# Moving row loads, combinations and first-stage pieces at the end of a kernel's ramp

## The chip, the cores and the metric

The kernel runs on one core of one Trainium2 chip. The metric is device microseconds of one execution. A core has a matrix engine (TensorE, PE in the profile), a vector engine (VectorE, DVE), a scalar engine (ScalarE, ACT), GpSimd (POOL) and a sync engine (SyncE, SP) that only issues transfers. ScalarE and GpSimd issue transfers too, each through its own queue. Each engine works its instructions off in order and waits for others by semaphores. TensorE writes to PSUM; the others work from PSUM or SBUF, except GpSimd, which in this kernel works from SBUF to SBUF.

## The reference

Two blocks follow each other. The first is a global filter: a real Fourier transform along the sequence of 3008, a product with a complex filter per frequency and channel, and the inverse transform. The second is a gated two-layer network on 24064 tokens.

```python
B, S, C, D_FF = 8, 3008, 256, 2048
X = np.fft.rfft(x, axis=1)                       # x: (8, 3008, 256)
y = np.fft.irfft(X * (filt_r + 1j * filt_i), n=S, axis=1)
t = y.reshape(B * S, C)
h = t @ w_in                                     # (24064, 2048)
out = (h * (1 / (1 + np.exp(-h)))) @ w_out       # (24064, 256)
```

`w_in` and `w_out` arrive as 64-bit floats (each is a float32 array times a numpy float64 scalar), so the kernel has to turn their words into 32-bit floats itself.

## The kernel before

**Transform.** S is split as 47 times 64 and the transform of each of the eight batches runs in stages on TensorE: a first stage over 94 rows (matmuls into tiles named pa, or pf for later batches), a twiddle stage (`forward`, tiles pb), the filter product on VectorE (`products`), an inverse twiddle stage (`inverse`, tiles pc) and a last stage (`stage3`, tiles pd) that leaves y with channels in partitions. Between stages the data is turned round through memory in HBM: the tiles q go out to d2 and come back as the tile t4, which `stage3` reads. For batch 0 that tile is a part of the not yet used weight tile w_t. Its rows come in three pieces, `load_t4_rows(k)` for k = 0, 1, 2, two transfers of 256 KB each; piece k needs the q stores of groups 2k and 2k+1. Group 4 is produced last.

**Network.** Both matrix products use a seven-product scheme on 2 by 2 blocks. A pair is 512 (or 480) tokens; each pair takes eight steps, one for each double block jp of the weights. `hidden(step)` gives seven matmuls (tiles px, pyz), copies of px to abc and the gating to g; `project(step - 1)` gives seven matmuls from g into acc. A loop over steps and eight rounds hands them out alternately, and `put(step, round, ...)` places every other piece of work into that sequence. With matmuls alone a step takes about 6.1 us, 14 matmuls of 0.43 us. The whole order of instructions is thus written out by hand; each engine gets its own in-order stream from it. Transfers by SP and ScalarE take one of eight completion semaphores in turn, and one that takes a semaphore still in use first waits for the earlier transfer on it, whichever queue that was on. GpSimd's transfers have another eight.

**Weights.** For each of the 16 weight blocks j, `weights` loads 512 KB of 64-bit words. `split` takes exponent and mantissa bits apart (two VectorE tensor_scalar instructions) and converts them (two ScalarE activations, four for j = 0, 2, 6), `rounded` rounds and sets the sign (three on VectorE), `placed` multiplies both into w_t. For each pair of blocks, `combine_weights` forms the sums of the seven-product scheme: four instructions of 256 elements per partition, on VectorE.

**The ramp.** Everything before step 0 is the ramp: transform of batch 0 and weight blocks 0 to 8. Its end is the stretch of the script from `inverse(2)` on: groups 3, 5 and 4 of the inverse stage, then the first two of eight first-stage pieces of batch 1 (`second["stage1"](u, False)`, tile pa, two 512-wide matmuls each, evicted by ScalarE and stored by GpSimd in `store_rows`), then 14 filler matmuls (`idle_wide`) whose result nobody reads, then `stage3` for groups 0 to 3. The other six first-stage pieces stand in steps 1 to 6. A one-column copy by GpSimd into the tile `gate` keeps the two row stores behind the placing of block 8.

In the steps, weight block j (9 to 15) has split, rounding and, for some, a combination after round 1 of step j - 9, and placing after round 5. The first-stage piece of batch 1 stands after round 3. Outputs go out through SP.

Of the kernel before, what the change touches and what calls it, by code (L numbers as in the profile page):

```python
# [46 lines left out]
FP32 = mybir.dt.float32  # L47
U32 = mybir.dt.uint32
AFT = mybir.ActivationFunctionType
ALU = mybir.AluOpType  # L50
# [120 lines left out]
def kernel(  # L171
# [59 lines left out]
    gate = cpool.tile([128, 1], FP32)  # L231
    x_all = xpool.tile([128, 2, 2, 2 * C], FP32)
    x_t = [x_all[:, i] for i in range(2)]

# [33 lines left out]
    def spectral(b):  # L268
# [257 lines left out]
        def rows_first(g):  # L526

            if g in (2, 3):
                room = t4pool.tile([128, 4, C], FP32, name=f"q_{b}_{g}", tag="t4")
                tiles = room[:, 0:2], room[:, 2:4]  # L530
            else:
                tiles = [pool.tile([128, 2, C], FP32, name=f"q_{b}_{g}_{i}", tag=tag) for i, (pool, tag) in
                         enumerate(((zpool, "z"),) * 2 if g == NG - 1 else ((qpool, "q"), (opool, "o")))]
            for i, qt in enumerate(tiles):
                copy, queue = (nc.scalar.copy, nc.scalar) if i == 0 or g < 4 else (nc.vector.tensor_copy, nc.sync)
                copy(out=qt, in_=halves[g][i])
                a0 = 8 * g + 4 * i
                queue.dma_start(out=d2[a0:a0 + 4].rearrange("a n h c -> (a n) h c"), in_=qt)
# [19 lines left out]
            for h in range(2):  # L558
                nc.sync.dma_start(out=t4s[g][64 * h:64 * h + 2 * NS], in_=d2[:, 4 * g:4 * g + 4, h, :])

        def load_t4_rows(k):

            first, by = SPREAD[k]
            for h in range(2):
                nc.sync.dma_start(out=us["t4"][64 * h + first:64 * h + first + 15 * by + 1:by],
                                  in_=d2[16 * k:16 * k + 16, 0:16, h, :])

        def stage3(g, home=None):
# [48 lines left out]
    def plan(b, part):  # L617
# [1 line left out]
        at = STEPS * b  # L619

        if b == 1:
            for u in range(2, 8):
                put(at + u - 49, 3, part["stage1"], u)
        else:
            put(at - 72, 0, part["reverse_x"])
            for f, step, load, places in ((0, -56, -66, ((-60, 3), (-60, 5), (-59, 5), (-58, 5))),
# [299 lines left out]
    def split_weights(*js):  # L926

        for j in js:
            words = raws[j].rearrange("p w (n t) -> p (w n) t", t=2)
# [8 lines left out]
            else:  # L938
# [5 lines left out]
            raws[j] = lo, hi, e, m, ef, mf, ends[0].bitcast(FP32), ends[1].bitcast(FP32), ends[1]  # L944
            v.tensor_scalar(out=e, in0=hi, scalar1=20, scalar2=0x7ff,
                            op0=ALU.logical_shift_right, op1=ALU.bitwise_and)
            nc.scalar.activation(out=ef, in_=e, func=AFT.Relu, bias=bias_t[:, 0:1])
            v.tensor_scalar(out=m, in0=hi, scalar1=0xfffff, scalar2=None, op0=ALU.bitwise_and)
# [50 lines left out]
    def weights(*js, queue=None):  # L999
        for j in js:  # L1000
            if wide:
                load_weights(j, queue)

    def split(*js):
        if wide:
            split_weights(*js)
# [75 lines left out]
    for k in range(16):  # L1082
        part["stage1_first"](k, 1)
        if k < 12:
            part["stage1_first"](k + 4, 0)
    second["load_x"](0)
    second["load_x"](1)
    weights(6, 7, 8)
    part["forward"](0, fill=4)
    placed(0, 1)  # L1090
    for g in range(1, 4):
# [18 lines left out]
    inverse(1)  # L1110
    products(3)
    part["forward"](5)
    part["load_t4_rows"](0)
    products(4)
    inverse(2)
    products(5)
    inverse(3)
    split(4, 5)
    combine_weights(0)
    inverse(5)  # L1120
    placed(2, 3)
    inverse(4)
    part["load_t4_rows"](1)
    part["load_t4_rows"](2)
    weights(9)
    split(6, 7)
    rounded(4, 5)
    split(8)
    for u in range(2):
        second["stage1"](u, False)  # L1130
    placed(4, 5)
    rounded(6, 7)
    placed(6, 7)
    rounded(8)
    placed(8)
    gp.tensor_copy(out=gate, in_=w_t[:, 4, A11, 0, 0:1])
    for u in range(2):
        second["store_rows"](u)
    idle_wide(14)
    for g in range(4):  # L1140
        part["stage3"](g)
    nc.sync.dma_start(out=wi_t, in_=wi_dram.ap())
    second["load_x"](2)
    weights(10, 11, 12)
    second["load_x"](3)
    weights(13)
    early[0] = None
    plan_rest(0, part)
    for g in (4, 5):
# [86 lines left out]
```

## Time and profile before

| | |
|---|---|
| runs | 2579.97, 2580.51 and 2583.06 us, median 2580.51 |
| profiled execution | 2580.21 us, span 2578.4 us |
| TensorE | 2554.4 us busy (99%), clock granted 0.995 on average |
| VectorE, ScalarE, GpSimd | 1664.1, 1086.4 and 420.2 us busy |
| TensorE from 55.5 to 70 us | 10.03 of 14.5 us busy |
| TensorE from 100 to 140 us | 39.81 of 40 us busy |

In the profile, "L580" is a line of the kernel, "px<-ty,w_t" names the tile written and the tiles read, and "x64" the number of records; a float32 matmul leaves two records. In a timeline each line is start, duration, engine, line, operation and count, and in brackets the idle time before it and what ended it. The chain is the work that ended last, followed back from the end; in order of time it gives start, duration and what. A line for a stretch of time gives the busy time of PE, weight load (PEld), DVE, ACT and POOL with their counts, then the granted TensorE clock (1.00 is full), the share of time in which the DMA engines were busy, and GB/s.

### The profile page before, as it was taken

How to read it: one execution, taken by the hardware profiler on the slowest of the kernel's cores; microseconds unless marked ns; L12 is line 12 of the kernel's file. 1: busy time of each engine (PE TensorE's matmuls, PEld its weight loads, DVE VectorE, ACT ScalarE, POOL GpSimd, SP SyncE). 2: the span in 40 equal slices, each digit the busy share in tenths (PEclk: the TensorE clock that was granted, in tenths of full speed). 3: DMA queues.
4: the chain of work that ended last, by engine and by line, in shares of the span. 5: the costliest groups of instructions: out<-in, count | busy, mean ns of one | idle time of the engine just before them, and what ended most of it. 6: DMA issues, size and time to landing. Idle time of an engine off the chain costs nothing.

```text
span 2578.4 us, 48112 instructions
## 1 busy us (share of the span) xinstructions
PE 2554.4 (99%) x18852; PEld 2197.4 (85%) x18852; DVE 1664.1 (65%) x3587; ACT 1086.4 (42%) x3011; POOL 420.2 (16%) x668
## 2 busy tenths in 40 slices
PE   9899999999999999999999999999999999999998
PEld 6688888888888888888888888988888888888987
DVE  7766666666666666666666666666666666555554
ACT  3544444444444444434444434444444444444443
POOL 2211111121112111311122111211121112101101
PEclk9899999999999999999999999999999999999999
DMA  9521232222222222222223222331232311210011
GB/s 290 159 60 50 71 79 63 60 64 75 60 63 69 70 62 58 76 73 64 64 60 87 51 66 58 80 80 46 66 80 64 73 41 29 63 19 16 9 17 16
DMA packets 200443, 171.08 MB, mean 66 GB/s; under 512 B 122100, under 2 KB 174180, under 8 KB 199428
## 3 DMA queue, kind: packets, MB, share of 16 engines
q1 hardware_dynamic: 179080, 117.85, 19.8%
q0 software_dynamic: 16768, 44.13, 5.4%
q10 hardware_dynamic: 4368, 6.03, 0.8%
q8 instruction: 148, 2.42, 0.4%
q14 instruction: 79, 0.65, 0.1%
HBM read 96.07 MB, written 81.26 MB: 69 GB/s over the span
## 4 chain that ended last, share of the span: by engine, by line
PE 97%; DMA 2%; DVE 0%; ACT 0%; issue 0%; ACTq 0%; SPq 0%; DVEq 0%
PE acc L813 44%; PE px L750 26%; PE pyz L750 19%; PE pd L580 3%; PE pb L457 2%; PE pc L500 2%; PE pf L424 1%; PE pa L344 0%; DMA w_t<-in_x_dram 0%; PE pc L522 0%; DMA w_t<-d 0%; PE pa L335 0%; DMA d_t<-d_tbl 0%; DMA e_t<-e_tbl 0%; DMA filt<-in_filt_r_dram 0%; DMA d<-q 0%
## 5 line engine op out<-in xcount | busy, mean ns | idle before, releaser
L813 PE MATMUL acc<-g,w_t 128*128 128x256 f32 (+1 forms) x5376 | 1508.8, 375 | 0.4 <-DVE g L721 0.4
L813 PEld LDWEIGHTS acc<-g,w_t 128*128 128x128 f32 x5376 | 1021.5, 190 | 115.8 <-DVE g L721 0.8
L721 DVE TENSOR_TENSOR g<-pyz,abc 128x256 f32<-128x256 f32 (+1 forms) x1152 | 479.3, 416 | 621.0 <-ACT abc L771 356.6
L721 DVE TENSOR_TENSOR g<-g 128x256 f32<-128x256 f32 (+3 forms) x1152 | 598.7, 520 | 196.6 <-ACT g L754 183.4
L750 PE MATMUL px<-ty,w_t 128*128 128x256 f32 (+1 forms) x2304 | 679.3, 377 | 1.1 <-ACT abc L765 0.6
L754 ACT ACTIVATE g<-g 128x256 f32<-128x256 f32 (+1 forms) x1152 | 472.9, 410 | 249.7 <-DVE g L721 249.7
L750 PEld LDWEIGHTS px<-ty,w_t 128*128 128x128 f32 x2304 | 432.7, 190 | 65.0 <-issue 6.2
L721 POOL TENSOR_TENSOR s<-s 128x256 f32<-128x256 f32 (+1 forms) x329 | 254.8, 791 | 1416.4 <-DVE s L833 1393.8
L750 PE MATMUL pyz<-y,w_t 128*128 128x256 f32 (+1 forms) x1536 | 454.0, 377 | 0.0
L750 PEld LDWEIGHTS pyz<-y,w_t 128*128 128x128 f32 x1536 | 284.0, 190 | 47.2 <-DVE g L721 7.1
L765 ACT COPY abc<-px 128x256 f32<-128x256 f32 (+1 forms) x384 | 141.1, 368 | 373.0 <-PE px L750 373.0
L771 ACT COPY abc<-px 128x256 f32<-128x256 f32 (+1 forms) x384 | 141.5, 369 | 338.7 <-PE px L750 337.7
L754 ACT ACTIVATE g<-px 128x256 f32<-128x256 f32 (+1 forms) x384 | 145.8, 380 | 300.7 <-PE px L750 300.7
L750 PE MATMUL px<-y,w_t 128*128 128x256 f32 (+1 forms) x768 | 232.6, 385 | 0.8 <-DVE y L594 0.8
L750 PE MATMUL pyz<-ty,w_t 128*128 128x256 f32 (+1 forms) x768 | 225.7, 376 | 0.2 <-DVE g L721 0.2
L750 PEld LDWEIGHTS px<-y,w_t 128*128 128x128 f32 x768 | 140.4, 190 | 33.9 <-DVE y L600 6.7
L750 PEld LDWEIGHTS pyz<-ty,w_t 128*128 128x128 f32 x768 | 144.6, 190 | 18.7 <-DVE g L721 1.0
L758 ACT COPY abc<-px 128x256 f32<-128x256 f32 (+1 forms) x384 | 135.4, 353 | 54.1 <-PE px L750 54.1
L580 PEld LDWEIGHTS pd<-wi_t,t 48*64 48x64 f32 x3840 | 61.2, 135 | 25.9 <-ACT g L754 16.4
L436 POOL DMA_DIRECT2D d<-tf x144 | 71.4, 502 | 37.0 <-DVE tf L432 29.0
L863 DVE STREAM_TRANSPOSE o<-s 128x256 f32<-128x256 f32 x192 | 73.9, 423 | 1.5 <-issue 1.0
L833 ACT COPY s<-acc 128x512 f32<-128x512 f32 (+1 forms) x94 | 54.2, 577 | 47.6 <-PE acc L813 47.6
(136 smaller groups left out, 1261.6 us busy)
## 6 DMA issues: line engine op xcount, KB each, us to landing
t<-d SPq DMA_DIRECT2D x120, 192.0 KB
t<-d SPq DMA_DIRECT2D x84, 256.0 KB
d<-q POOLq DMA_DIRECT2D x84, 256.0 KB, 2.6
out_dram<-o SPq DMA_DIRECT2D x636, 32.0 KB
d<-tf POOLq DMA_DIRECT2D x144, 96.0 KB, 2.9
xr<-in_x_dram SPq DMA_DIRECT2D x6, 1472.0 KB
x_all<-in_x_dram SPq DMA_DIRECT2D x72, 96.0 KB
x_all<-xr SPq DMA_DIRECT2D x72, 96.0 KB
```

The source lines that it names most:

```text
L436: nc.gpsimd.dma_start(out=d1[k // 2, :, k % 2, n0:n0 + 4], in_=us["tf"][32 * k:32 * k + NS].rearrange("p q n c -> p (q n) c"))
L457: nc.tensor.matmul(out=ps[k][32 * j:32 * j + 32, ri, :], lhsT=d_t[rows, 4 * g + at, ri, :], rhs=rhs, start=True, stop=True)
L580: nc.tensor.matmul(out=ps[h][c0:c0 + 64, cb, i, :], lhsT=t4[rows, i, 128 * cb + c0:128 * cb + c0 + 64], rhs=wi_t[rows, :], start=True, sto ...
L721: eng.tensor_tensor(out=out, in0=in0, in1=in1, op=op)
L750: nc.tensor.matmul(out=out, lhsT=w_t[:, jp, c, 0], rhs=rhs, start=start, stop=True, skip_group_check=True)
L754: nc.scalar.activation(out=g[:, k, 0:n], in_=g[:, k, 0:n] if src is None else src, func=AFT.Silu)
L758: nc.scalar.copy(out=sums[:, 0, 0:n], in_=xo)
L765: nc.scalar.copy(out=sums[:, 1, 0:n], in_=xo)
L771: nc.scalar.copy(out=sums[:, 2, 0:n], in_=xo)
L813: nc.tensor.matmul(out=acc[pair][i][:, h, 0:n], lhsT=w_t[:, jp, c, 1], rhs=g[:, k, 0:n], start=(jp == 0 and h == 0), stop=last, skip_group ...
L833: copy(out=s[:, 2 * i:2 * i + 2, 0:n], in_=acc[pair][i][:, :, 0:n])
L863: v.transpose(out=o[:, :, h, :], in_=results[pair][:, ((2, 6), (4, 1))[chunk][h], :])
```

## The change

At the end of the ramp:

- The loads of the first two x pieces of batch 1 and of weight block 8 leave the place before `forward(0)`. Block 8 is loaded with block 9, after the last rows; the x pieces are loaded after `stage3`, where pieces 2 and 3 were.
- The first two first-stage pieces, with their evictions, their stores and `gate`, leave the ramp. All eight pieces of batch 1 now stand after round 3 of steps 1 to 8.
- Rows k = 0 and 1 are issued by GpSimd in place of SP; k = 2 stays on SP.
- Blocks 2 to 5 are placed by GpSimd, and the combinations of pairs 0 to 3 are made by GpSimd.
- `split` falls into `bits` (VectorE) and `converted` (ScalarE), so that the conversions of blocks 4 and 5 stand behind the q copies.
- The second q copy of group 3 goes to VectorE and its store to SP.
- The filler grows from 14 to 22 matmuls.

In the steps:

- Block 8 is prepared in step 0, and all blocks get new places (`turns`): split at a turn, rounding two rounds later, placing four rounds later. The turns are, as step and round, (0, 1), (1, 0), (1, 7), (2, 6), (3, 5), (4, 4), (5, 1) and (6, 0) for blocks 8 to 15.
- The combinations of pairs 4 to 7 are made by GpSimd, four rounds after the turn of the second block.

```diff
-                copy, queue = (nc.scalar.copy, nc.scalar) if i == 0 or g < 4 else (nc.vector.tensor_copy, nc.sync)
+                copy, queue = (nc.scalar.copy, nc.scalar) if i == 0 or g < 3 else (nc.vector.tensor_copy, nc.sync)
...
-        def load_t4_rows(k):
+        def load_t4_rows(k, queue=None):
...
-                nc.sync.dma_start(out=us["t4"][64 * h + first:64 * h + first + 15 * by + 1:by],
+                (queue or nc.sync).dma_start(out=us["t4"][64 * h + first:64 * h + first + 15 * by + 1:by],
...
-            for u in range(2, 8):
-                put(at + u - 49, 3, part["stage1"], u)
+            for u in range(8):
+                put(at + u - 47, 3, part["stage1"], u)
...
-    second["load_x"](0)
-    second["load_x"](1)
-    weights(6, 7, 8)
+    weights(6, 7)
...
-    part["load_t4_rows"](0)
     products(4)
+    combine_weights(0, eng=gp)
     inverse(2)
+    part["load_t4_rows"](0, nc.gpsimd)
     products(5)
     inverse(3)
-    split(4, 5)
-    combine_weights(0)
+    bits(4, 5)
+    placed(2, 3, eng=gp)
+    part["load_t4_rows"](1, nc.gpsimd)
     inverse(5)
-    placed(2, 3)
+    bits(6, 7)
     inverse(4)
-    part["load_t4_rows"](1)
+    converted(4, 5)
     part["load_t4_rows"](2)
-    weights(9)
-    split(6, 7)
+    weights(8, 9)
+    combine_weights(1, eng=gp)
+    converted(6, 7)
     rounded(4, 5)
-    split(8)
-    for u in range(2):
-        second["stage1"](u, False)
-    placed(4, 5)
+    placed(4, 5, eng=gp)
+    combine_weights(2, eng=gp)
     rounded(6, 7)
     placed(6, 7)
-    rounded(8)
-    placed(8)
-    gp.tensor_copy(out=gate, in_=w_t[:, 4, A11, 0, 0:1])
-    for u in range(2):
-        second["store_rows"](u)
-    idle_wide(14)
+    combine_weights(3, eng=gp)
+    idle_wide(22)
     for g in range(4):
         part["stage3"](g)
     nc.sync.dma_start(out=wi_t, in_=wi_dram.ap())
-    second["load_x"](2)
+    second["load_x"](0)
     weights(10, 11, 12)
-    second["load_x"](3)
-    weights(13)
+    second["load_x"](1)
...
-    for j in range(9, NJ):
-        if j < 12:
-            put(j - 9, 1, lambda j=j: (split(j), combine_weights(j - 8), rounded(j)))
-        else:
-            put(j - 9, 1, lambda j=j: (split(j), rounded(j)))
-        put(j - 9, 5, placed, j)
+    turns = {8: (0, 1), 9: (1, 0), 10: (1, 7), 11: (2, 6), 12: (3, 5), 13: (4, 4), 14: (5, 1), 15: (6, 0)}
+    for j, (step, rnd) in turns.items():
+        turn = step * ROUNDS + rnd
+        put(0, turn, split, j)
+        put(0, turn + 2, rounded, j)
+        put(0, turn + 4, placed, j)
         if j % 2:
-            put(*((j - 8, 5) if j < 15 else (j - 9, 6)), combine_weights, j // 2, 0)
-            put(*{13: (j - 8, 7), 15: (j - 8, 1)}.get(j, (j - 7, 5)), combine_weights, j // 2, 1)
-        if j < 11:
-            put(j - 9, 1, weights, j + 5)
+            put(0, turn + 4, lambda jp=j // 2: combine_weights(jp, eng=gp))
+        if j in (8, 9, 10):
+            put(0, turn + 4, weights, j + 5)
```

More of the change, by code (lines that the diff above doesn't have):

```diff
@@ L230 @@
     bias_t = cpool.tile([128, 5], FP32)
-    gate = cpool.tile([128, 1], FP32)
     x_all = xpool.tile([128, 2, 2, 2 * C], FP32)
@@ L924, in load_weights, with bits_of_weights @@
         raws[j] = raw
-    def split_weights(*js):
+    def bits_of_weights(*js):
         for j in js:
@@ L946, in split_weights, with convert_weights @@
                             op0=ALU.logical_shift_right, op1=ALU.bitwise_and)
+            v.tensor_scalar(out=m, in0=hi, scalar1=0xfffff, scalar2=None, op0=ALU.bitwise_and)
+    def convert_weights(*js):
+        for j in js:
+            _, _, e, m, ef, mf, *_ = raws[j]
             nc.scalar.activation(out=ef, in_=e, func=AFT.Relu, bias=bias_t[:, 0:1])
-            v.tensor_scalar(out=m, in0=hi, scalar1=0xfffff, scalar2=None, op0=ALU.bitwise_and)
             nc.scalar.activation(out=mf, in_=m, func=AFT.Identity, scale=2.0 ** -20, bias=1.0)
@@ L1002, in weights, with bits, converted @@
                 load_weights(j, queue)
+    def bits(*js):
+        if wide:
+            bits_of_weights(*js)
+    def converted(*js):
+        if wide:
+            convert_weights(*js)
     def split(*js):
-        if wide:
-            split_weights(*js)
+        bits(*js)
+        converted(*js)
     def rounded(*js):
```

## The prediction

> **What bounds the kernel now.** I read the page first: one core, TensorE (PE) 99% busy, chain 97% PE. So a change near the start is worth the time by which the first dense TensorE stretch moves, less any TensorE work added later. Its table of slices shows one dent, in slice 2. I then asked for the chain in order of time there, and for TensorE's timeline:
>
> ```profile
> PE 97%; DMA 2%; DVE 0%; ACT 0%; issue 0%; ACTq 0%; SPq 0%; DVEq 0%
> ...
> 55.31 5.42 DMA w_t<-d
> 60.81 5.07 DMA d<-q
> 66.61 4.10 DMA w_t<-d
> 70.85 7.12 PE pd L580 x254
> ...
> 59.13 6.21 PE L1037 MATMUL idle<-d_t,wx_t 96*128 96x256 f32 x28
> 69.81 0.42 PE L580 MATMUL pd<-wi_t,w_t 48*64 48x47 f32 x2 [4.47 <-DMA w_t<-d]
> 70.85 7.07 PE L580 MATMUL pd<-wi_t,w_t 48*64 48x47 f32 x254 [0.62 <-DMA w_t<-d]
> 78.69 1.19 PE L750 MATMUL px<-y,w_t 128*128 128x256 f32 x2 [0.77 <-DVE y L594]
> 87.58 0.60 PE L813 MATMUL acc<-g,w_t 128*128 128x256 f32 x2
> ```
>
> Three transfers stand in a row: rows k=0 into w_t, the last q store, rows k=2. TensorE idles from 65.34 to 69.81. ScalarE's timeline says why the store was late, and the stretch by stretch view what the gap does to the clock (column before the DMA share):
>
> ```profile
> 58.25 0.58 ACT L536 COPY q<-pc 128x512 f32<-128x512 f32 x1 [0.40 <-ACT q L536]
> 60.81 0.33 ACTq L538 DMA_DIRECT2D d<-q  x1
> 61.18 0.72 ACT L947 ACTIVATE w_t<-w_t,bias_t 128x512 f32<-128x512 uint32 x1 [2.35 <-DMA w_t<-d]
> ...
> 66.00:67.00 1.00, 0.00 (x0) 0.00 (x0) 1.00 (x2) 1.00 (x4) 0.00 (x0) 1.00 0.00 0
> 68.00:69.00 1.00, 0.00 (x0) 0.00 (x0) 0.90 (x3) 0.00 (x0) 0.00 (x0) 0.50 1.00 276
> 86.00:87.00 1.00, 1.00 (x4) 0.66 (x3) 0.09 (x2) 0.69 (x2) 0.00 (x0) 0.50 1.16 343
> 88.00:89.00 1.00, 1.00 (x6) 0.88 (x5) 0.86 (x2) 0.21 (x1) 0.00 (x0) 1.00 1.06 228
> ```
>
> The copy was done at 58.83, but its store issued at 60.81, when rows k=0 had landed: in the built program both use the same completion semaphore. Finer stretches put the half clock from 67.1 to 87.5. After that TensorE is full: 39.81 of the 40 us from 100 to 140.
>
> **What the Trainium skill says.** "TensorE: Matmul & The Clock Gate", Part 1: the clock halves after an idle window of about 3.4 us that runs free of the kernel, and returns after a busy one. The trace agrees on the free run (67.1 to 87.5 is six windows), not on a whole idle window: it fell 1.8 us after the last matmul. "SBUF — State Buffer", Who interferes with whom: a VectorE instruction with two SBUF inputs, or a tensor_scalar in its fast mode, and a GpSimd instruction that reads SBUF lock each other out for its whole length. The trace agrees: the tensor_scalar at 49.92 took 1.15 us while GpSimd added until 50.79, its like afterwards 0.41. "GPSIMD Engine Reference", 4.1 Engine selection: two-input elementwise work is about twice slower there; here 0.69 to 0.75 against 0.37 us. "DMA: Bandwidth & Descriptors", SWDGE vs HWDGE vs iDMA: GpSimd's DMAs build descriptors in software in SBUF and can be held by VectorE's fast mode. No run yet shows such a row load; the d<-q stores by POOL land in 2.6 us, the nearest row.
>
> **The change part by part**, against the profiled execution (span 2578.4, its time 2580.2; the median, 2580.51, is 2.1 above the span).
>
> (a) Fewer loads before the rows. x 0 and 1 (768 KB) and weight block 8 (512 KB) leave SP's queue at 39 to 50. ScalarE's store of q_1_0 waited 3.3 us there for an x load (issue at 49.22 after a copy done at 45.92); that goes. TensorE still ends pc at about 55.5: GpSimd's additions end at 50.79 as before.
>
> (b) Store order. q_4_0's store needs no rows load any more: pc ends 55.6, copy 0.6, issue about 56.3 in place of 60.81. But q_4_1, on VectorE and then SP, now follows bits(6,7), four tensor_scalars of 0.41, while GpSimd places blocks 2 and 3. Bounds: VectorE always first, copy done at 57; GpSimd always first, at 59.7. I take 58.4. Landing 2.6 later, 61.0. The second store of q_3 also goes to VectorE and SP (0.6, before bits(4,5)); the conversions of blocks 4 and 5 move behind the stores on ScalarE, 56.7 in place of 55.0, so rounding and placing of blocks 4 to 7 end near 70 on VectorE and GpSimd. They are due in steps 2 and 3, past 85: nothing, unless they hold VectorE's y copies at 69.7, which (f) takes in.
>
> (c) Rows. k=0 issues behind four combinations on GpSimd: 50.8 + 4 x 0.72 = 53.7, then two issues. k=1 behind the four placings, 58 to 60. SP's k=2 needs the q_4 stores: 61.0, second issue 0.66 later, 4.1 to land (both as now): 65.8. Three row loads and four stores share the DMA engines (share 1.00 or more from 57 to 63.5, down to 123 GB/s while k=0 moves), so 0.7 more: pd starts at 66.5 (bounds 65.3, where the filler ends, and 69). Behind k=2 on SP stand only the loads of blocks 8 and 9, due from step 0 on, past 71; behind k=0 on GpSimd the placings and k=1, counted above.
>
> (d) Filler. 22 x 0.444 (6.21/14) = 9.8 us from 55.5 ends at 65.3, where pa and 14 did. A gap of 1.2 us stays.
>
> (e) pd at full clock: four times the 1.08 us of 64 later records, 4.4, in place of 8.1 (69.81 to 77.92); then 0.8 to px as now.
>
> (f) Step 0, px to first acc, 8.9 us at half clock. With 0.43 us matmuls and the same ScalarE and VectorE chain (ty 1.6, g 0.4, bits 0.7, two activations 1.2, copies) I get 6.7. VectorE loses its four combinations, but GpSimd's combination 3 now runs beside ty: 0.7 for the lock. 7.4.
>
> First acc: 66.5 + 4.4 + 0.8 + 7.4 = 79.1 against 87.58: **8.5 gained**.
>
> (g) pa 0 and 1, hidden in the wait until now, run in full steps: 2 x 1.73 = **3.5 lost**. Their x loads go behind wi_t, some 11 us before use, as x 2 and 3 do now: nothing. Row stores follow two steps later; they land about a step before load_t2 at step 10: nothing, the cover is about 3 us.
>
> (h) Weight work at new places in the steps. It was after round 1, where pa covered it. The two activations (1.2 us) wait for VectorE's bits, and ScalarE's next copy waits behind them. Block 10 now comes after round 7. In today's step the g activation runs at 95.90, the px copy at 96.22, and the next matmul into px at 96.89:
>
> ```profile
> 95.90 0.42 ACT L754 ACTIVATE g<-g 128x256 f32<-128x256 f32 x1 [0.95 <-DVE g L721]
> 96.22 0.35 ACT L758 COPY abc<-px 128x256 f32<-128x256 f32 x1
> 96.89 0.59 PE L750 MATMUL px<-ty,w_t 128*128 128x256 f32 x2
> ```
>
> In the new order that copy has in front of it g[4:6] (0.69, VectorE), bits (0.4) and the activations (1.2): it ends near 98.5, so TensorE waits 1.7. Block 12, after round 5, delays the activation that reads px before the next step's first matmul (102.37 to about 103.5, needed at 103.03): 0.9. Block 13, after round 4, does the same, and its rounding (1.6) stands before the g1 addition: 1.2. Block 11 just fits; 8, 9, 14, 15 stay near round 0 or 1, under pa. Sum **3.8 lost**. TensorE has no slack to give these back.
>
> (i) Combinations of blocks 4 to 7 on GpSimd, 3.0 us each, need a step's lead; the last pair follows the row stores and leaves under 1 us. Nothing if covered.
>
> (j) Clock in pd and step 0. Step 0 at full clock keeps TensorE busy for less than half of some 3.4 us windows, about what the window before 67.1 held (1.6 of 3.4). A fall there costs some 2 us; slightly likelier than not, I count it.
>
> Sum: 8.5 - 3.5 - 3.8 - 2 = 0.8 us lost. On the median: **2581.3**. A measurement tells some 0.2% (5.2 us) from no change, so this is within it.
>
> **Rivals.** *Faster*: the waits of (h) are absorbed and the clock holds. For it: today's steps carry 6.5 us of VectorE work in 8 with no loss. Against: the order of instructions on ScalarE. 8.5 - 3.5, and 0.7 if GpSimd harms nothing: 5.0 to 5.7 gained, 2575. *Slower, by the clock*: rows land after about 67.2, and the clock halves before or in pd. For it: the slow row loads and (b)'s upper bound; today's half-clock pd, busy from 71 to 76, did not bring the clock back. Start 68.5, then pd and step 0 as now: 68.5 + 8.1 + 0.8 + 8.9 = 86.3, gain 1.3; less 7.3 it is 6 lost, 2586.5. It decides from 1.8 us of gap. *Slower, by the lock*: GpSimd's 16 combinations in the steps each hold VectorE up to 0.75 us when g additions are due; a third of them on the path add 4: 2585. *No effect of the queue change*: k=1 by GpSimd lands last, no sooner than today's k=2; it then runs like the clock rival.
>
> **How the numbers follow.** Forecast 0.50, faster 0.15, clock (with the late k=1) 0.22, lock 0.13. The forecast's own range is 2577 to 2585. About two thirds of the faster rival passes 5.2 us: faster 0.10. The two slow rivals, less their milder part, and a tail of the forecast give slower 0.34. Same takes the rest, 0.56. Range 2574.5 to 2589: from the faster case to late rows with the in-step waits of (h) doubled.
>
> **What would show it.** Right: a store of q at about 56 on ScalarE's queue; pd starting at 65.3 to 67.2 with 256 records in under 5 us; waits of TensorE on ACT abc at steps 2, 4 and 5; the pair after round 7 in front of a px copy. Wrong: no such waits, or GpSimd's rows landing last, or PEclk at 0.5 before pd, or VectorE instructions stretched to over 1 us in many steps.

## The result, and the profile after

The changed kernel takes 2593.09 us (median of five runs, 2590.73 to 2593.31). The kernel before took 2581.11 beside it (five runs, 2579.97 to 2583.06). The ratio is 1.0043, 95% interval 1.0029 to 1.0056: 11 to 12 us slower, outside the predicted range. The profiled span grew from 2578.4 to 2588.9 us, 10.5 us; the profiled execution of the changed kernel is the fastest of its five. Lines of the changed kernel are one lower than before (pd L579, px L749, acc L812, combinations L720).

The chain still is TensorE's, so the time is again the sum of what TensorE waits for and does at a lower clock. The page of the changed kernel, then its chain in order of time (start, duration, what):

```profile
PE 97%; DVE 1%; DMA 1%; ACT 0%; issue 0%; POOL 0%; DVEq 0%; SPq 0%; ACTq 0%
...
57.09 0.61 DVE q L535
57.70 0.02 issue
57.71 5.38 DMA d<-q
...
63.90 4.33 DMA w_t<-d
68.23 0.14 issue
68.36 7.12 PE pd L579 x254
```

The wait for rows k=0 ahead of the last store is gone: q_4_0 was stored at 55.15, without that wait, as forecast. But the last store, of q_4_1, took 5.38 us, and pd stands at 68.36. TensorE's timeline of the changed kernel shows the rest; the number in brackets is TensorE's wait, then who ended it:

```profile
67.11 0.41 PE L579 MATMUL pd<-wi_t,w_t 48*64 48x47 f32 x2 [2.91 <-DMA w_t<-d]
68.36 7.07 PE L579 MATMUL pd<-wi_t,w_t 48*64 48x47 f32 x254 [0.84 <-DMA w_t<-d]
76.20 1.19 PE L749 MATMUL px<-y,w_t 128*128 128x256 f32 x2 [0.77 <-DVE y L593]
...
83.70 0.59 PE L812 MATMUL acc<-g,w_t 128*128 128x256 f32 x2
...
95.95 0.67 PE L749 MATMUL px<-ty,w_t 128*128 128x256 f32 x2 [2.75 <-ACT abc L757]
...
107.99 0.70 PE L749 MATMUL pyz<-ty,w_t 128*128 128x256 f32 x2 [1.27 <-DVE g L720]
...
114.31 0.70 PE L749 MATMUL px<-y,w_t 128*128 128x256 f32 x2 [0.88 <-ACT g L753]
...
132.24 0.67 PE L749 MATMUL px<-ty,w_t 128*128 128x256 f32 x2 [1.58 <-ACT abc L764]
...
145.68 0.70 PE L749 MATMUL px<-ty,w_t 128*128 128x256 f32 x2 [0.55 <-POOL w_t L720]
```

Three readings. pd again takes 7.07 us for 254 records, the half-clock value of the kernel before. The first acc, which ends step 0, comes at 83.70 in place of 87.58, so the ramp gained 3.9 us and not 8.5. And the steps, which before had a single wait over 0.15 us (0.19, at 129.99), now have waits that sum to 9.1 us (2.75, 1.27, 0.88, 0.47, 0.69, 0.73, 0.18, 1.58, 0.55; the four that the fence leaves out are of the same kinds, in steps 4 and 5). Stretches of the changed kernel show the clock, the column before the DMA share:

```profile
66.00:67.00 1.00, 0.00 (x0) 0.00 (x0) 0.96 (x2) 0.00 (x0) 1.00 (x2) 0.76 1.10 241
68.00:69.00 1.00, 0.64 (x25) 0.67 (x28) 0.90 (x2) 0.00 (x0) 0.92 (x2) 0.50 1.03 362
...
80.00:81.00 1.00, 0.26 (x2) 0.24 (x2) 0.57 (x1) 0.97 (x3) 0.00 (x0) 0.91 1.01 338
...
90.42:93.83 3.41, 2.78 (x13) 2.07 (x12) 2.32 (x5) 1.10 (x3) 3.32 (x6) 1.00 0.93 290
93.83:97.24 3.41, 1.29 (x6) 1.19 (x7) 2.42 (x6) 2.19 (x5) 1.63 (x2) 1.00 0.18 72
97.24:100.66 3.42, 3.42 (x7) 1.75 (x6) 2.21 (x5) 0.58 (x2) 0.00 (x0) 0.50 0.00 0
```

The clock is halved from about 66.5 to 80.2, and once more in step 2, from 97.24 to 100.66, right after a window of 3.41 us that held most of the wait of 2.75 us: 3.4 us at half speed, 1.7 us of work lost.

What the weight work does to step 2 is seen in the timelines of three engines of the changed kernel, ScalarE first, then VectorE, then GpSimd:

```profile
94.05 0.72 ACT L951 ACTIVATE e<-e,bias_t 128x512 f32<-128x512 uint32 x1 [1.67 <-DVE e L944]
94.92 0.63 ACT L952 ACTIVATE m<-m 128x512 f32<-128x512 uint32 x1
95.45 0.35 ACT L757 COPY abc<-px 128x256 f32<-128x256 f32 x1
```

```profile
93.08 0.94 DVE L944 TENSOR_SCALAR e<-raw 128x512 uint32<-128x512 uint32 x1
93.94 0.94 DVE L946 TENSOR_SCALAR m<-raw 128x512 uint32<-128x512 uint32 x1
```

```profile
91.85 3.61 POOL L720 TENSOR_TENSOR w_t<-w_t 128x256 f32<-128x256 f32 x4
```

ScalarE's copy of px stands behind the two conversions of block 10, these behind VectorE's bits, and the bits took 0.94 us each beside GpSimd's combination of pair 4.

### The profile page after: what moved, and what is told of

Same layout as the page of the kernel before. It is cut to its first block, busy times and chain, and to the rows that moved or that the text cites. A ratio compares the mean times of both kernels' runs of the same rounds, so it can differ in the third digit from the quotient of the medians.

```text
span 2588.9 us, 48178 instructions
## 1 busy us (share of the span) xinstructions
PE 2560.1 (99%) x18868; PEld 2199.8 (85%) x18868; DVE 1665.0 (64%) x3548; ACT 1087.5 (42%) x3010; POOL 456.3 (18%) x711
## 4 chain that ended last, share of the span: by engine, by line
PE 97%; DVE 1%; DMA 1%; ACT 0%; issue 0%; POOL 0%; DVEq 0%; SPq 0%; ACTq 0%
PE acc L812 43%; PE px L749 26%; PE pyz L749 19%; PE pd L579 3%; PE pb L456 2%; PE pc L499 2%; PE pf L423 1%; PE pa L300 1%; PE pa L334 1%; PE idle L1042 1%; PE pc L521 1%; PE pa L343 0%; DVE g L720 0%; DMA d<-q 0%; DMA w_t<-d 0%
## 5 line engine op out<-in xcount | busy, mean ns | idle before, releaser
L812 PE MATMUL acc<-g,w_t 128*128 128x256 f32 (+1 forms) x5376 | 1509.2, 375 | 0.4 <-DVE g L720 0.4
L812 PEld LDWEIGHTS acc<-g,w_t 128*128 128x128 f32 x5376 | 1021.5, 190 | 115.7 <-DVE g L720 0.8
L720 DVE TENSOR_TENSOR g<-pyz,abc 128x256 f32<-128x256 f32 (+1 forms) x1152 | 479.8, 416 | 637.6 <-ACT abc L770 371.0
L720 DVE TENSOR_TENSOR g<-g 128x256 f32<-128x256 f32 (+3 forms) x1152 | 600.7, 521 | 197.5 <-ACT g L753 184.3
L749 PE MATMUL px<-ty,w_t 128*128 128x256 f32 (+1 forms) x2304 | 678.1, 376 | 6.1 <-ACT abc L757 2.8
L720 POOL TENSOR_TENSOR s<-s 128x256 f32<-128x256 f32 (+1 forms) x329 | 254.8, 792 | 1404.6 <-DVE s L832 1393.6
L749 PEld LDWEIGHTS px<-ty,w_t 128*128 128x128 f32 x2304 | 432.4, 190 | 71.1 <-issue 13.6
L749 PE MATMUL pyz<-y,w_t 128*128 128x256 f32 (+1 forms) x1536 | 453.3, 377 | 0.8 <-DVE g L720 0.7
L749 PEld LDWEIGHTS pyz<-y,w_t 128*128 128x128 f32 x1536 | 283.8, 189 | 47.5 <-DVE g L720 6.7
L749 PE MATMUL px<-y,w_t 128*128 128x256 f32 (+1 forms) x768 | 232.5, 384 | 2.3 <-ACT g L753 1.6
L749 PE MATMUL pyz<-ty,w_t 128*128 128x256 f32 (+1 forms) x768 | 226.2, 376 | 2.0 <-DVE g L720 1.9
L749 PEld LDWEIGHTS px<-y,w_t 128*128 128x128 f32 x768 | 140.0, 189 | 35.2 <-DVE y L599 5.8
L749 PEld LDWEIGHTS pyz<-ty,w_t 128*128 128x128 f32 x768 | 144.2, 190 | 22.1 <-DVE g L720 4.6
L579 PEld LDWEIGHTS pd<-wi_t,t 48*64 48x64 f32 x3840 | 61.3, 135 | 25.3 <-ACT g L753 16.4
```

What stands on the lines that cost most here:

```text
L579: nc.tensor.matmul(out=ps[h][c0:c0 + 64, cb, i, :], lhsT=t4[rows, i, 128 * cb + c0:128 * cb + c0 + 64], rhs=wi_t[rows, :], start=True, sto ...
L720: eng.tensor_tensor(out=out, in0=in0, in1=in1, op=op)
L749: nc.tensor.matmul(out=out, lhsT=w_t[:, jp, c, 0], rhs=rhs, start=start, stop=True, skip_group_check=True)
L812: nc.tensor.matmul(out=acc[pair][i][:, h, 0:n], lhsT=w_t[:, jp, c, 1], rhs=g[:, k, 0:n], start=(jp == 0 and h == 0), stop=last, skip_group ...
```

## The experiments

Fourteen kernels were run, each beside the kernel before, which gave medians of 2580.56 to 2581.11. "Steps" is the start of step 10 less the start of step 1 in TensorE's timeline (first px of a step).

| kernel | median us | ratio, 95% interval | first acc | steps |
|---|---|---|---|---|
| before | 2581.11 | | 87.58 | 67.34 |
| changed | 2593.09 | 1.0043 [1.0029, 1.0056] | 83.70 | 82.50 |
| e1_vector_combos | 2591.26 | 1.0041 [1.0026, 1.0056] | 84.64 | 81.65 |
| e2_steps_before | 2582.12 | 1.0005 [0.9996, 1.0014] | 86.36 | 69.98 |
| e5_before_turns_gpsimd | 2584.55 | 1.0015 [1.0008, 1.0022] | 87.09 | 72.88 |
| e10_block10_covered | 2589.27 | 1.0034 [1.0022, 1.0047] | 83.41 | 79.21 |
| e4_longer_filler | 2589.18 | 1.0034 [1.0022, 1.0046] | 82.46 | 81.55 |
| e3_before_filler | 2578.31 | 0.9989 [0.9983, 0.9996] | 85.68 | 67.96 |
| e6_rows_on_SP | 2593.82 | 1.0055 [1.0041, 1.0068] | 84.71 | 85.03 |
| e13_rows_after_store | 2595.66 | 1.0056 [1.0041, 1.0072] | 90.25 | 81.05 |
| e9_vector_alone_in_ramp | 2583.80 | 1.0012 [1.0006, 1.0019] | 89.48 | 70.99 |
| e7_steps_before_filler | 2581.64 | 1.0005 [0.9998, 1.0012] | 86.27 | 71.56 |
| e8_pa_in_ramp | 2580.93 | 0.9999 [0.9990, 1.0007] | 89.47 | 67.23 |
| e11_block8_early | 2581.56 | 1.0000 [0.9992, 1.0009] | 86.21 | 71.85 |
| e12_block8_early_pa_in_ramp | 2577.05 | 0.9987 [0.9980, 0.9993] | 87.91 | 68.62 |
| e14_best_longer_filler | 2577.52 | 0.9988 [0.9981, 0.9994] | 87.66 | 68.52 |

**The steps: turns or lock?** Two theories. "Order": the conversions stand in front of ScalarE's copies at turns that no pa piece covers. "Lock": GpSimd's combinations stretch VectorE's pieces. The first run takes GpSimd out and leaves the turns:

```diff
-            put(0, turn + 4, lambda jp=j // 2: combine_weights(jp, eng=gp))
+            put(0, turn + 4, lambda jp=j // 2: combine_weights(jp))
```

> The changed kernel, with the combinations of pairs 4 to 7 in the steps given back to VectorE, at the same turns; everything else stays. Steps 1 to 8 of the changed kernel lost about 12 us against the kernel before, where 3.8 were forecast. Theory 'lock': VectorE's pieces (bits 0.94 us each instead of 0.41, a g subtraction of 1.77) are stretched by GpSimd's combinations beside them; without these, bits take 0.41 again, the halved clock at 98 us goes, and 5 us or more come back: 2588 or less. Theory 'order': the conversions stand in front of ScalarE's copies at turns that no pa piece covers, and VectorE now has 1.5 us more work per pair of blocks; the waits at steps 2, 4 and 5 stay and at most 2 us come back, or some are lost: 2591 to 2596.

The median came 1.8 us lower, but the ratio (1.0041 against 1.0043) hardly moved. VectorE of this kernel in step 2, then TensorE in steps 2, 3 and 5:

```profile
95.53 0.42 DVE L944 TENSOR_SCALAR e<-raw 128x512 uint32<-128x512 uint32 x1
95.87 0.42 DVE L946 TENSOR_SCALAR m<-raw 128x512 uint32<-128x512 uint32 x1
```

```profile
97.63 0.67 PE L749 MATMUL px<-ty,w_t 128*128 128x256 f32 x2 [2.00 <-ACT abc L757]
...
107.99 0.70 PE L749 MATMUL pyz<-ty,w_t 128*128 128x256 f32 x2 [1.28 <-DVE g L720]
...
129.23 0.70 PE L749 MATMUL pyz<-ty,w_t 128*128 128x256 f32 x2 [1.78 <-DVE g L720]
```

The bits are back at 0.42 us, so GpSimd did stretch them. But the waits sum to 8.75 us (0.55, 2.00, 1.28, 0.69, 0.48, 0.70, 0.73, 1.78, 0.54) against 9.1: in sum it makes no difference here which engine makes the combinations; the waits move. The one in step 2 shrank from 2.75 to 2.00, and in step 5 one of 1.78, for a g addition on VectorE, stands in place of the 1.58. A half-clock window came here too, in step 1 (83.1 to 86.6) and not in step 2.

The second run has the steps of the kernel before on the changed ramp, with block 8 in the ramp (first diff, against the changed kernel). The third has the same places with GpSimd's combinations (second diff, against the second run):

```diff
     combine_weights(3, eng=gp)
+    split(8)
+    rounded(8)
+    placed(8)
...
-    for j, (step, rnd) in turns.items():
...
+    for j in range(9, NJ):
+        put(j - 9, 1, lambda j=j: (split(j), rounded(j)))
+        put(j - 9, 5, placed, j)
```

```diff
-            put(*((j - 8, 5) if j < 15 else (j - 9, 6)), combine_weights, j // 2, 0)
+            put(*((j - 8, 5) if j < 15 else (j - 9, 6)), lambda jp=j // 2: combine_weights(jp, 0, eng=gp))
```

> The changed kernel's ramp (rows by GpSimd, combinations of pairs 0 to 3 by GpSimd) with block 8 prepared in the ramp, and the schedule of the kernel before for the weight work of blocks 9 to 15 in the steps, combinations on VectorE; all pa pieces stay in steps 1 to 8. If the steps' loss is the weight work's turns and GpSimd's combinations, steps 1 to 8 take 7.8 to 8.2 us each and some 11 us come back: ramp 3.9 gained, pa 3.5 lost, 2579 to 2582. If the two added pa pieces or the clock of the ramp cost the steps more than 3.5 us, the time stays over 2585.

> As the run with the steps of the kernel before, but the combinations of pairs 4 to 7 stay on GpSimd, in halves, at the places of the kernel before. Theory 'lock': steps with a combination are longer by 1 to 3 us each as in the changed kernel, sum 4 or more: 2585 to 2590. Theory 'order': GpSimd's combinations cost nothing at places that pa covers: within 1.5 us of the run with VectorE's combinations, 2579 to 2583.

With the old places 11 us come back (2582.12), and the only wait over 0.15 us from step 1 to step 10 is one of 0.19 us, as in the kernel before. The steps take 69.98 us, 12.5 less than in the changed kernel with the same eight pa pieces in them; against the 67.34 of before, with six pieces, 2.6 more. The two added pieces alone make steps 7 and 8 3.4 us longer (15.82 against 12.43); steps 1 to 3, where combinations 1 to 3 no longer stand, are 0.8 shorter, about half of it because in the kernel before the half clock lasts into step 1. With GpSimd's combinations at those places the median is 2.4 us higher and the steps 2.9, of which about 1.2 is a half-clock window in step 1, after a step 0 that has the same work in both kernels; the result lies between the two theories' ranges. The waits on TensorE's timeline of the third run show one cause, combinations that come late:

```profile
130.08 0.70 PE L749 MATMUL px<-ty,w_t 128*128 128x256 f32 x2 [0.63 <-POOL w_t L720]
...
139.09 0.70 PE L749 MATMUL px<-ty,w_t 128*128 128x256 f32 x2 [0.62 <-POOL w_t L720]
```

One turn alone, from round 7 of step 1 to round 1 of step 2:

```diff
-    turns = {8: (0, 1), 9: (1, 0), 10: (1, 7), ...
+    turns = {8: (0, 1), 9: (1, 0), 10: (2, 1), ...
```

> The changed kernel with one turn moved: block 10 starts at round 1 of step 2 instead of round 7 of step 1. Nothing else changes. If the weight work's turn is what holds TensorE (conversions in front of ScalarE's copy of px), the wait of 2.75 us in step 2 and the half clock after it (97.4 to 100.7, some 1.7 us) go: 4 us faster than the changed kernel, 2588 to 2590. If GpSimd's combination of pair 4, which runs there too, is what holds VectorE, 2 us or more of the wait stay: 2591 to 2593.

2589.27, 3.8 us below the changed kernel's median. TensorE of this kernel in steps 2 and 3; the half clock after 97.2 is gone too:

```profile
97.15 0.67 PE L749 MATMUL px<-ty,w_t 128*128 128x256 f32 x2 [0.80 <-ACT abc L764]
...
104.39 0.70 PE L749 MATMUL pyz<-ty,w_t 128*128 128x256 f32 x2 [1.28 <-DVE g L720]
```

One block in another place is worth a third of the loss. So the turns carry most of it. GpSimd's combinations cost a fifth of it at the old places (e5 against e2); at the turns no run separates their lock from the work that VectorE has without them.

Whether the wait in step 2 costs clock as well depends on where the clock's windows lie. The kernel with more filler (e4, below) has the same wait, 2.77 us before 95.08, but there it falls across two windows, and the clock holds through both:

```profile
90.54:93.95 3.41, 1.77 (x9) 1.21 (x7) 2.85 (x4) 1.14 (x2) 3.32 (x5) 1.00 0.85 286
93.95:97.37 3.42, 2.29 (x10) 1.88 (x11) 2.40 (x7) 1.58 (x4) 0.64 (x1) 1.00 0.00 0
```

Its step 2 takes 10.8 us (first px to first px) against 12.45 in the changed kernel and 7.9 in e2; in e13 it is 10.8 too, with a wait of 2.75.

**The ramp: what makes the store late?** The row loads back on SP, at the same places of the script:

```diff
-    part["load_t4_rows"](0, nc.gpsimd)
+    part["load_t4_rows"](0)
...
-    part["load_t4_rows"](1, nc.gpsimd)
+    part["load_t4_rows"](1)
```

> The changed kernel with the rows k=0 and k=1 issued by SP at the same places in the program, as the kernel before does, in place of GpSimd's queue. Combinations and placings stay on GpSimd. The store of q_4_1 took 5.38 us to land in the changed kernel instead of the 2.6 assumed, with GpSimd's two row loads in flight. Theory 'queue': GpSimd's row loads are what delays it: with SP's the store lands in about 2.6 to 3.5 us and pd starts 2 us or more earlier, if SP's queue is not held at k=0 or k=1. Theory 'traffic': any two row loads beside the stores share the DMA engines: the store still takes about 5 us, pd starts within 1 us of the changed kernel's 68.4 and the time stays within 2 us of it, 2591 to 2595.

"Traffic" holds: 2593.82, and pd's 254 records start at 68.76. The store, now behind rows k=1 on SP, was issued from 59.2 on, and the rows k=2 that wait for it followed at 63.86. The last store, issued at 59.83, thus took about 4.0 us, with only rows k=1 beside it. So the queue is not the cause in the main; whether it makes the step from 4.0 to 5.38, or the rows k=0 that were still moving in the changed kernel, is not shown. (The steps are longest here since two half-clock windows, 97.0 to 103.8, fell in step 2.) Next, all weight work of the ramp on VectorE, which shortens the bits ahead of the copy of q_4_1 (against e2; combinations 1 to 3 go to steps 0 to 2 as before, and rows k=1 stand before bits(4, 5)):

```diff
-    combine_weights(0, eng=gp)
...
-    placed(2, 3, eng=gp)
...
-    bits(6, 7)
     inverse(4)
...
     part["load_t4_rows"](2)
+    combine_weights(0)
+    placed(2, 3)
     weights(8, 9)
+    split(6, 7)
...
+    placed(8)
-    idle_wide(22)
+    idle_wide(30)
```

> The changed kernel's row loads by GpSimd and its order of stores, but all weight work of the ramp back on VectorE: combinations 0 and the placings of blocks 2 to 8 in the ramp, combinations 1 to 3 in steps 0 to 2, blocks 9 to 15 in the steps, as in the kernel before; 30 idle groups; all pa pieces in the steps. GpSimd only issues row loads there. Theory 'lock in the ramp': the eight pieces of bits took 0.8 to 0.97 us beside GpSimd and take 0.41 to 0.75 now, q_4_1 is copied at 56 instead of 57.7, the rows land at 66 to 67.5 instead of 68.3, VectorE is free when pd ends (y copies 0.8 after pd instead of 4.3 in the run with 30 groups and block 8 in the ramp), first acc at 82 to 83.5: 2577 to 2579.5. Rival: VectorE alone is as slow as VectorE held by GpSimd, y copies are late again, 2580.5 to 2583.

The copy did come 1.6 us earlier, at 56.07, with bits of 0.42. It gained nothing: the chain of this kernel shows the store landing at 63.68, against 63.09 in the changed kernel. But GpSimd, free of weight work, also issued rows k=1 earlier, at 54.93 in place of 57.50, so all four row transfers were ahead of the store. The chain, then TensorE's timeline:

```profile
56.07 0.03 DVE w_t L720
56.10 7.58 DMA d<-q
```

```profile
73.41 0.91 PE L579 MATMUL pd<-wi_t,w_t 48*64 48x47 f32 x47 [1.43 <-issue]
80.58 1.19 PE L749 MATMUL px<-y,w_t 128*128 128x256 f32 x2 [6.25 <-DVE y L593]
```

The 6.25 us ahead of px are another matter: block 8's load stood behind the rows on SP, landed at 69.75 and left VectorE idle for 7.1 us, with the y copies behind it (VectorE's copies of pd to y, which px reads). So the time came out near the rival's (2583.80), but not for its reason. Last, the row loads taken out of the store's way, by putting both behind GpSimd's combinations of pair 1:

```diff
-    part["load_t4_rows"](0, nc.gpsimd)
...
-    part["load_t4_rows"](1, nc.gpsimd)
...
     combine_weights(1, eng=gp)
+    part["load_t4_rows"](0, nc.gpsimd)
+    part["load_t4_rows"](1, nc.gpsimd)
```

> The changed kernel with GpSimd's two row loads (k=0, k=1) moved behind its combinations of pair 1, so that they are issued at about 60 to 62 instead of 53 and 57.5, and the store of q_4_1 (issued at about 57.7) has the DMA engines nearly to itself. Nothing else changes. If the row loads in flight are what stretches the store, it lands in 2.6 to 3.5 us instead of 5.38, at 60 to 61.5; the three row loads then run together, and pd starts at 66 to 69: within 3 us of the changed kernel. If the store's time has another cause (its own descriptors, the write to DRAM, the other stores), it lands in 5 us or more again and pd starts at 68.5 or later.

SP's queue of this kernel: the store at 58.54, and at 60.67 the rows k=2, which wait for that store.

```profile
58.54 0.32 SPq L537 DMA_DIRECT2D d<-q  x1
60.67 1.28 SPq L564 DMA_DIRECT2D w_t<-d  x2
62.00 0.59 SPq L919 DMA_DIRECT2D raw<-in_moe_w_in_dram  x1
```

The same 256 KB store now landed in 2.1 us. Only the row loads were moved, so these are what stretches it: in the changed kernel the DMA engines were busy all of 57.7 to 63.1 (share 1.00, 255 GB/s), and GpSimd's queue moved 0.82 of the 1.58 MB between 57 and 64. The forecast of pd at 66 to 69 missed: the rows, now all at once and beside four weight loads, took 10.74 us, and pd's main part started at 73.40.

**The ramp: the clock.** More filler, so that TensorE has no gap before pd, in the changed kernel and in the kernel before:

```diff
-    idle_wide(22)
+    idle_wide(30)
```

```diff
-    idle_wide(14)
+    idle_wide(25)
```

> The changed kernel with 30 instead of 22 idle matmul groups, so that the filler ends about 68.0 us instead of 64.2 and leaves TensorE no gap before pd. If the gap of 3 us is what halves the clock, TensorE keeps full speed in pd (256 records in 4.4 us instead of 8.1) and step 0: first acc about 79 to 81 instead of 83.7, and the time falls by 3 to 5 us to 2588 to 2590. If pd's short matmuls and step 0's waits throttle the clock anyway, the clock falls one window later and at most 1.5 us come back.

> The kernel before, with 25 instead of 14 idle matmul groups at the end of the ramp: the filler ends about 70.2 us instead of 65.3, after the rows k=2 have landed, and TensorE has no gap. Nothing else changes. In the changed kernel eight more groups kept the clock at full through pd and most of step 0, moved half speed to about three us of step 1, and the kernel was 3.9 us faster. Theory 'gap': the same here, pd in 5 instead of 8.1 us and step 0 shorter: 3 to 5 us faster than the kernel before, 2576 to 2578. Rival: the filler's matmuls themselves delay pd (no gain, 2580 to 2582).

Both gained: 3.9 us at the changed kernel's median, and 2.7 for the kernel before (0.11%, interval 0.04 to 0.17%), which beats both kernels by filler alone. In the first the time was as expected, the first acc, at 82.46, later than the 79 to 81. TensorE in the first of them, and then its clock in three stretches of a window's length (busy PE first, clock before the DMA share):

```profile
67.86 3.62 PE L579 MATMUL pd<-wi_t,w_t 48*64 48x47 f32 x209
72.43 0.91 PE L579 MATMUL pd<-wi_t,w_t 48*64 48x47 f32 x47 [0.95 <-issue]
74.12 0.67 PE L749 MATMUL px<-y,w_t 128*128 128x256 f32 x2 [0.78 <-DVE y L593]
```

```profile
73.48:76.89 3.41, 1.86 (x7) 1.07 (x7) 3.24 (x6) 0.75 (x2) 2.19 (x3) 1.00 0.44 101
76.89:80.30 3.41, 1.69 (x6) 0.80 (x6) 2.40 (x6) 2.19 (x5) 0.00 (x0) 1.00 1.04 319
80.30:83.70 3.40, 3.40 (x9) 2.47 (x8) 2.21 (x6) 1.46 (x4) 0.00 (x0) 0.50 1.07 320
```

pd takes 5.5 us in place of 8.3, and the half clock shrinks to one window (80.3 to 83.7). It follows a window in which step 0 kept TensorE busy for 1.69 of 3.41 us. The kernel before came out 0.3 us above its forecast; in its profiled execution the rows landed 0.9 later than in that of the kernel before, and the half clock still came for one window, at 83.5.

**Towards a better kernel.** The rest combines these: the old steps, 30 groups and the placings of blocks 6 and 7 on GpSimd; then pa 0 and 1 back in the ramp; then both again with the load of block 8 moved ahead of the last store on SP; then the last of these with more filler.

e7, against e2:

```diff
-    placed(6, 7)
+    placed(6, 7, eng=gp)
...
-    idle_wide(22)
+    idle_wide(30)
```

e8, against e7 (the other six pa pieces stand in steps 1 to 6 again):

```diff
+    second["load_x"](0)
+    second["load_x"](1)
     weights(6, 7)
...
+    for u in range(2):
+        second["stage1"](u, False)
+    for u in range(2):
+        second["store_rows"](u)
-    idle_wide(30)
+    idle_wide(22)
```

e11 and e12, against e7 and e8:

```diff
     inverse(3)
+    weights(8)
...
-    weights(8, 9)
+    weights(9)
```

e14, against e12:

```diff
-    idle_wide(22)
+    idle_wide(28)
```

> As the run with the steps of the kernel before on the changed ramp (2582.12), with the placings of blocks 6 and 7 on GpSimd, so that VectorE is free for the y copies 2 us earlier, and 30 instead of 22 idle groups. If the ramp's loss is the clock plus the late y copies there, the sum is 2582.1 - 3.9 - 2: 2575 to 2578. If GpSimd's longer work holds VectorE in step 0 by the lock, or the halved clock only moves into step 1, half of this or less: 2579 to 2582.

> As the run before it in this list, with pa 0 and 1 of the second batch back in the ramp, in the wait for the rows, as in the kernel before, their x loads ahead of the weight blocks on SP's queue, and 22 idle groups. The two pieces cost 1.73 us each in full steps: 3.5 us faster than that run, 2571.5 to 2574.5, if the x loads do not delay the q stores on the way to pd. If they do by 2 us or more, no gain over it: 2575 to 2578.

> As the run with 30 groups, block 8 in the ramp and the placings of blocks 6 and 7 on GpSimd (2581.64), with the load of block 8 alone moved ahead on SP's queue, before the store of q_4_1 and the rows k=2, so that it lands by about 56 instead of 69.5. If the late y copies (4.28 us of TensorE's wait after pd) were due to that load and not to the lock, they come 0.8 us after pd, the clock holds into step 0, first acc at 81.5 to 83 instead of 86.3: 2577 to 2579. If VectorE's pieces beside GpSimd were the reason, most of the 4.28 us stays: 2580.5 to 2582.5.

> As the run before it in this list, with pa 0 and 1 of the second batch in the ramp (their x loads ahead on SP's queue) and 22 idle groups. In the like run with the late load of block 8 pd waited 3.46 us for ScalarE's copy of pa, which stood behind the conversions of block 8. With the early load this wait goes, and the steps lose 3.5 us less than with pa in them: 2574.5 to 2577, less than either kernel. If the x loads delay the rows by 1.5 us or more, as they may have done there (pd at 69.7), 2577 to 2579.

> As the run with block 8's load early and pa 0 and 1 in the ramp (2577.05), with 28 instead of 22 idle groups, so that the filler ends at about 71.5 instead of 68.9 and no gap stands before pd. If the gap halves the clock in pd, pd takes 5.2 instead of 8.1 us and 2 to 4 us are gained: 2573 to 2575.5. If the late y copies then hold TensorE instead (VectorE is busy with block 8 until 76.5), or the half clock moves into steps 0 and 1, at most 1 us: 2576 to 2577.5.

The wait that e7, e8 and e11 (in this order) still have, on TensorE's timeline, one line from each kernel:

```profile
78.26 1.19 PE L749 MATMUL px<-y,w_t 128*128 128x256 f32 x2 [4.28 <-DVE y L593]
```

```profile
74.29 5.36 PE L579 MATMUL pd<-wi_t,w_t 48*64 48x47 f32 x190 [3.46 <-ACT t L350]
```

```profile
76.84 1.19 PE L749 MATMUL px<-y,w_t 128*128 128x256 f32 x2 [2.70 <-DVE y L593]
```

In e7 a filler that keeps the clock buys nothing, because VectorE, late with block 8, makes the y copies 4.28 us after pd. In e8 the same lateness holds the conversions of block 8 on ScalarE and behind them the eviction of pa; the time missed both of its ranges. The early load takes 1.6 of the 4.28 us away (e11), less than forecast, and the time does not move, as the half clock then holds from 75.7 to 89.4 and the first acc comes at 86.21 in place of 86.27. The remaining 2.70 go with VectorE's pieces beside GpSimd, bits of 0.95 and roundings of up to 1.1, which no run took apart. In e12 the wait for ScalarE is gone; at 2577.05 it beats the changed kernel by 16 us and the kernel before by 0.13% (interval 0.07 to 0.20%). That is not clear of what filler alone gave the kernel before (e3, 2578.31). Where its gain lies is not shown: the profiled execution was the longest of its 21 runs (2580.24 us), with a span of 2578.5 like that of the kernel before, and it reaches step 10 1.6 us later than that one does. More filler on top (e14) lets most of pd run at full clock, but moves the half clock into steps 0 and 1 (77.2 to 90.8): first acc comes at 87.66 in place of 87.91, and the time is the same within what can be measured.

## Why the prediction was wrong

The forecast was 0.8 us lost; the time rose by some 12, of which the profiled executions show 10.5 (11.6 at the start of step 10). Two of its steps failed, both to the slow side. (h), the waits in the steps, weighs most: 12.5 us where 3.8 stood. (b), the landing of the last store, with what followed from it, left the ramp a gain of 3.9 where 8.5, less the 2 of (j), stood. Of the signs named, the early store and the pair after round 7 in front of a px copy came; pd's 256 records in under 5 us did not, and the half clock stood before pd, a sign of being wrong.

- **(a), (d)** Right on the stores; pc ended 1.1 us earlier than taken (54.44, not 55.5). So the filler ended at 64.20, not 65.3, and the gap grew by that much.
- **(b)** The first failed step. Its copy was well bounded (done at 57.70; 58.4 taken). "Landing 2.6 later" was wrong: 5.38. The 2.6 was taken from GpSimd's q stores of later batches, whose traffic is another; the prediction's own first fence had the nearest row, this very store, at 5.07 us with rows k=1 beside it. e13 shows the 2.1 us of a store alone, e6 that the issuing queue changes pd by only 0.4, e9 that an earlier copy gains nothing while the row loads stay ahead of the store.
- **(c)** The 4.1 us of rows k=2 were right (4.33). With (b)'s error they landed at 68.23 in place of 65.8, or 66.5 with the 0.7 set aside for sharing. That is past the 67.2 at which the clock rival was said to decide, and it did: the gap was 2.91 us.
- **(e)** Failed in consequence: pd took 8.3 us, not 4.4. e4 shows 5.5 where no gap is left. **(f)** came out in number, 7.5 against 7.4, but by luck: it supposed full clock, and 4.0 of the 7.5 us ran at half clock (until 80.2), while e4, with full clock for the first 6.2 us, took 8.3. Together: pd's first record 0.6 late, pd and the wait behind it 3.9 longer, step 0 0.1 longer: 4.6 less than 8.5, the 3.9 seen.
- **(g)** Right: 3.5 taken, 3.4 measured where the two pieces stand (steps 7 and 8 of e2 against before).
- **(h)** The second failed step. The method, who stands in front of ScalarE's px copy, found the right places: block 10 in step 2, block 12 at the next step's first px (0.88 for 0.9), block 13 in step 5 (1.6 in three waits for 1.2). The sizes were too small. Block 10 waited 2.75 for 1.7, in part because its bits took 0.94 each (with bits of 0.42, in e1, it was still 2.00), and as the clock's windows lay this set off a half-clock window of 1.7, so one block cost 4.4 (e10 took 3.8 of it back). No term of (h) had a clock. Block 11, said to just fit, cost 1.27: its conversions stand in front of ScalarE's g activation (104.81), and behind that its rounding, 1.7 us on VectorE (105.85 to 107.52), in front of a g addition. Block 14, said to lie under pa, cost 1.58: its bits, at 129.36 and 130.22, took 0.94 each beside GpSimd's combination of pair 6, and outlasted pa. In all 12.5 us were lost in steps 1 to 9 (against e2) where 3.8 stood: 8.9 more in waits, 1.7 of clock, and 1.9 that lie around the waits. TensorE starts slowly after each: the matmul at 107.99 starts 1.87 us after the one before it where 0.43 is usual, so 1.44 are lost for the 1.27 in brackets, and the next one follows after 0.54.
- **(i)** "Nothing if covered" failed: the last pair was late (0.55), as its own warning said, and at the old places GpSimd's combinations still cost 2.4 us (e5), where TensorE waits for the combinations themselves (0.63 and 0.62). The Trainium skill, "SBUF — State Buffer", Who interferes with whom, has GpSimd and a VectorE tensor_scalar in its fast mode lock each other out, and the trace agrees: bits of 0.94 beside GpSimd, 0.42 without. But the lock rival alone is not what happened: without GpSimd's combinations in the steps the loss stays (e1).
- **(j)** Its 2 us for a clock fall were booked in pd and step 0. The clock was lost there at its full price and once more in step 2.

The slower rival by the clock had the right mechanism and, at 2586.5, half the loss; it used the 7.3 us of (g) and (h) as they stood. The range doubled (h), to 7.6, and stopped there.

## What to carry to other kernels

When a step's cost is a transfer, take its duration from the transfer itself under the traffic of that moment, not from the median of its kind elsewhere. When work is put at a new place in a full, in-order pipeline, list for every engine that it uses what stands behind it there, with cover or without: two conversions of some 1.3 us in front of the wrong copy cost a wait of 2.75 us, and 4.4 with the clock; two rounds later the wait there was 0.80. A gain in one transfer or copy is only a gain if the next thing in line (rows, clock, y copies) is not late as well.

## What the runs showed of the hardware

- The clock fell after windows of 3.41 us in which TensorE was busy for 1.29 (changed kernel, step 2), 1.66 (kernel before, 63.68 to 67.09) and 1.69 us (e4, step 0). The Trainium skill, "TensorE: Matmul & The Clock Gate", Part 1, speaks of an idle window; none of these was idle. The busy time of the profile draws no sharp line: the clock held after 1.69 (e1, step 2) and 1.86 (e4, step 0), but fell after 1.87 (e5, step 0), and after 1.93 to 2.02 in step 0 of e1, e6 and e7. What decides between is not shown. One line that held (e1) and one that fell (e5):

```profile
93.39:96.80 3.41, 1.69 (x7) 0.83 (x5) 2.42 (x7) 1.23 (x3) 0.08 (x1) 1.00 0.72 266
81.97:85.38 3.41, 1.87 (x7) 0.71 (x6) 2.40 (x6) 2.09 (x6) 0.00 (x0) 1.00 1.04 326
```

- In every run the stretches at half clock before step 10 are whole multiples of 3.41 us (20.5 in the kernel before, 13.65 and 3.41 in the changed kernel), and they begin at other places of the program from run to run. So the same wait can cost clock or not: 2.75 us, most of it in one window, cost 4.4 (changed kernel); 2.77 and 2.75 across two windows cost no clock (e4, e13).
- A window that the short matmuls of pd filled at half clock (3.41 of 3.41 us busy as the profile counts it, changed kernel, 69.94 to 73.35) did not bring the full clock back; it returned at 80.2.
- A 256 KB store to HBM landed in 2.1 us alone (e13), and beside row loads of 256 KB each in about 4.0 (by SP, e6), 5.1 (by SP, kernel before) and 5.4 to 7.6 (by GpSimd, changed kernel and e9).
- Beside back-to-back GpSimd additions a VectorE tensor_scalar of 512 elements per partition took 0.93 to 0.97 us in place of 0.42.
- Filler matmuls that keep the clock up before a stage of short matmuls were worth 2.7 us in the kernel before, where 3 to 5 were expected: in its profiled execution step 0, busy for about half a window (1.72 of 3.41 us), lost the clock once all the same.
